# One step of a matmul order moved between two halves of a convolution, and an evacuation placed ahead of the last sine

## The chip, the cores and the metric

The kernel runs on one core of a Trainium2 chip. The metric is the device time of one execution in microseconds (us); the figure for the kernel before is the median of three runs. A separate, profiled execution gives the page and the trace that all readings come from.

## What is computed

The reference first runs a causal convolution along the sequence. Each of 8 heads has 7 taps, normalised by a softmax, and each head covers 24 of the 192 channels. Then comes a two-layer network with the activation h * cos(h):

```python
# x (8, 4096, 192), weight (8, 7); w = softmax(weight) along the taps
out = einsum('hk,bskhg->bshg', w, x_unf)     # x_unf: windows of 7 rows, zero-padded ahead
x = out.reshape(32768, 192)
h = x @ w_in                                  # 192 -> 2048, product 1
g = h * cos(h)
result = g @ w_out                            # 2048 -> 192, product 2
```

## The kernel before

The 32768 rows are worked in 64 tiles of 512 rows; two tiles make a unit of 1024 rows, for which rows are loaded and convolved together. All instructions are emitted in an order that is written out by hand, in strings of short tokens, one string per tile for TensorE (with what hangs on it) and one for ScalarE.

*Product 1.* `hJ` (J from 0 to 7) is `mm1`, line 405: six matmuls, 512 columns wide, that fill two banks of PSUM with a block `h`. TensorE's rows are split into two halves that work side by side, so matmuls come in pairs. The blocks come from a ring of three (`h_pool`), which the convolution shares.

*The activation.* `sJ` is `gcu`, lines 409 to 417: ScalarE writes the sine of h + pi/2 into `cs`, and VectorE multiplies it by `h` into `g`, which frees the block of the ring.

*Product 2.* `mN` emits N steps of `mm2_step`, line 452. A tile has 64 steps, of two matmuls each with 192 columns, one on each half of the rows. They run about one tile behind product 1. They add into two output banks, one for each pair of row blocks (`o_p` and `o_q`), and `q` and `p` mark the half and the end of a tile's 64 steps. At the half, the two row halves exchange banks.

*Evacuation.* `P` (ScalarE), and `Q` (VectorE) or `A` (ScalarE), copy the two output banks of the finished tile to `o_sb` (`evac`, line 470). `O` stores a tile whose two copies have been emitted (line 473), on SyncE's queue.

*The convolution.* In the steady order each tile convolves half of the heads of a unit ahead (`conv_part`, line 220; matmuls of line 196). `c1` emits four matmuls (two pairs), `c2` four more that add into the same two banks with the row halves exchanged. The second group must not start before the first has ended. This is done by a `Turn` (lines 163 to 174): an empty instruction on SyncE (seen in the profile as L168) waits for the first group, and the second group waits for it:

```python
            turn.mark(mm(1, 0), mm(3, 1))
            yield
            turn.wait(mm(2, 0), mm(0, 1))
```

`ec1` and `ec2` are ScalarE's copies of the two banks (line 211). `D` doubles the copied rows on GpSimd (line 264), `X` transposes them by DMA (line 275, SyncE's queue), `Y` mends the edges of the row blocks on GpSimd (lines 297 to 309), `K` casts loaded rows to bf16 on GpSimd (line 184), and `L` issues the loads of a unit (lines 75 and 69, SyncE's queue).

*Which tile uses which string.* Tiles 0 to 3 use `PE_FIRST` and `ACT_FIRST`, tiles 4 to 62 `PE_ORDER` and `ACT_ORDER`, and tile 63 `PE_LAST` and `ACT_LAST`. The convolution ends with tile 59; afterwards `c1` and `c2` emit nothing. A token of ScalarE's string is emitted as soon as it stands first and what it needs has been emitted on TensorE's side: `sJ` needs `hJ`, `P`, `Q` and `A` need `p`. In tile 63, product 2 of that tile itself starts with the `m7` after `h7`. Its 64 steps take row blocks in another order (`LAST_HALF`): 14 steps go to two blocks of the ring, 14 to the output banks `o_p` and `o_q`, then two and two for the last block of `g`, and then the second half.

Of the kernel before, what the change touches and what calls it, by code (L numbers as in the profile page):

```python
# [16 lines left out]
def kernel(  # L17
# [9 lines left out]
    B, S, D = x.shape  # L27
    H, K = weight.shape
# [191 lines left out]
    def conv_part(u, c, banks, whole=False):  # L220


        ps = banks()
        nb = UB + (u == 1)
        sides = [slice(0, 64), slice(64, 128)]

        def mm(i, rows, **flags):
            return conv_mm(u, c, ps, i, sides[rows], 0, nb, **{"start": False, "stop": False, **flags})

        if whole:  # L230
            for i in range(4):
                conv_mm(u, c, ps, i, slice(0, 128), 0, nb, start=i % 2 == 0, stop=i % 2 == 1)
            if u == 2 and c == 0:
                spread_taps(ps[1][:, UB * 2 * G : UB * 2 * G + K])
            yield
        else:
            mm(0, 0, start=True)
            mm(2, 1, start=True)
            turn = Turn()
# [3 lines that stand above are left out]
            mm(3, 0, stop=True)  # L243
            mm(1, 1, stop=True)
        yield
        if u not in ct_tiles:
            ct_tiles[u] = ct_pool.tile([128, UB + 1, NC, 2, 64], BF16, name="ct")
        for b in range(2):
            conv_out(u, c, ps, 0, 0, nb, nc.scalar.copy, banks=(b,))
            if b and u == 2 and c == 0:  # L250
                nc.scalar.copy(tap, ps[1][:, UB * 2 * G : UB * 2 * G + K])
            if b:
                have.add(("conv", u, c))
            yield
# [76 lines left out]
    for i, k in enumerate("DPDPDPDPDPDPDPAA"):  # L331
        q, rows = divmod(i, 4)
# [152 lines left out]

    PE_ORDER = "m11 h0 m4 h1 m6 h2 m7 q Y K h3 m7 h4 m7 c1 m3 c2 X L m6 h5 m9 p h6 D O h7 m4"
    ACT_ORDER = "s0 s1 s2 s3 s4 ec1 ec2 Q s5 P s6 s7"

    PE_FIRST = ["h0a L2 h0b h1 h2 h3 K1 W0 d11 d21 h4 h5 c11 W1 L3 c21 h6 h7 K2",
# [6 lines left out]
                "s0 s1 s2 s3 s4 Q s5 P s6 s7"]  # L498

    PE_LAST = "m10 h0 m3 h1 m13 h2 m2 q h3 m10 h4 m3 h5 m7 h6 m12 p h7 O m7"  # L500
    ACT_LAST = "s0 s1 s2 s3 s4 s5 s6 P s7 A"

    HALVES = {"": (0, NB), "a": (0, NB // 2), "b": (NB // 2, NB), "l": (0, NB // 2), "r": (NB // 2, NB)}
    conv = {}
# [4 lines left out]
    for t in range(NT + 1):  # L509
        u, second = divmod(t, TPU)  # L510
        cu = u + TPU
        if t >= 2 * TPU:
            conv["c"] = conv_part(cu, second, ring_banks) if cu < NU else iter(())
        pe = PE_LAST if t == NT - 1 else "m%d p" % (2 * STEPS * NT - step) if t == NT else PE_ORDER if t >= len(PE_FIRST) else PE_FIRST[t]
        act = ACT_LAST if t == NT - 1 else ACT_ORDER if t >= len(ACT_FIRST) else ACT_FIRST[t]
        act, h = act.split(), {}
# [95 lines left out]
```

## Time and profile before

| what | value |
|---|---|
| median of 3 runs | 714.65 us (714.59 to 715.40) |
| the profiled execution's own time | 715.43 us |
| its span on the core | 713.7 us |
| granted TensorE clock | 1.0 |
| TensorE matmuls, busy | 704.7 us (99%) |
| VectorE, busy | 638.4 us (89%) |
| ScalarE, busy | 599.3 us (84%) |
| GpSimd, busy | 303.4 us (43%) |
| matmuls of product 2 (L452), busy | 427.4 us, 8128 of 243 ns |
| matmuls of product 1 (L405), busy | 405.3 us, 3078 of 376 ns |
| matmuls of the convolution (L196), busy | 39.7 us, 472 of 245 ns |

The span runs from the first to the last instruction on the core; the execution's own time is longer by what lies around it. The durations of matmuls overlap each other, so the mean duration of one is several times its share of the time; the distance between the starts of two says what one costs. In the rows of a timeline stand the start and the length in us, the engine (PE is TensorE, PEld its weight loads, ACT ScalarE, DVE VectorE, POOL GpSimd, SP SyncE), the line of the kernel, the operation, what it writes and reads, and how many instructions the row merges; in square brackets stand idle time of the engine ahead of the row and who ended it.

### The profile page before, as it was taken

How to read it: one execution, taken by the hardware profiler on the slowest of the kernel's cores; microseconds unless marked ns; L12 is line 12 of the kernel's file. 1: busy time of each engine (PE TensorE's matmuls, PEld its weight loads, DVE VectorE, ACT ScalarE, POOL GpSimd, SP SyncE). 2: the span in 40 equal slices, each digit the busy share in tenths (PEclk: the TensorE clock that was granted, in tenths of full speed). 3: DMA queues.
4: the chain of work that ended last, by engine and by line, in shares of the span. 5: the costliest groups of instructions: out<-in, count | busy, mean ns of one | idle time of the engine just before them, and what ended most of it. 6: DMA issues, size and time to landing. Idle time of an engine off the chain costs nothing.

```text
span 713.7 us, 26519 instructions
## 1 busy us (share of the span) xinstructions
PE 704.7 (99%) x11826; PEld 512.3 (72%) x11826; DVE 638.4 (89%) x599; ACT 599.3 (84%) x717; POOL 303.4 (43%) x307
## 2 busy tenths in 40 slices
PE   8899999999999999999999999999999999999997
PEld 4677777777777777777777777777777777777776
DVE  6789998999899999989989989989998999999996
ACT  7788888888888888888888888888888888888875
POOL 6533554443553434544434544245544335532400
PEclk9999999999999999999999999999999999999999
DMA  9674445445356454355364465453453553643411
GB/s 234 165 197 71 125 120 146 97 123 138 94 134 145 79 141 119 101 145 127 93 146 89 130 146 106 113 138 101 127 145 84 136 111 114 141 95 76 96 46 46
DMA packets 183713, 85.25 MB, mean 119 GB/s; under 512 B 111664, under 2 KB 183216, under 8 KB 183600
## 3 DMA queue, kind: packets, MB, share of 16 engines
q1 hardware_dynamic: 182888, 82.59, 47.7%
q8 instruction: 92, 1.51, 0.9%
q0 software_dynamic: 416, 0.79, 0.6%
q10 hardware_dynamic: 296, 0.20, 0.1%
q14 instruction: 21, 0.17, 0.1%
HBM read 31.36 MB, written 25.17 MB: 79 GB/s over the span
## 4 chain that ended last, share of the span: by engine, by line
PE 96%; DVE 1%; ACT 1%; POOL 1%; issue 0%; POOLq 0%; DVEq 0%; SPq 0%
PE o_ps L452 47%; PE h L405 46%; PE h L196 3%; ACT cs L413 1%; DVE g L417 1%; POOL x_bf L184 0%; DVE band L333 0%; PE h L452 0%; PE h L363 0%; ACT ct L355 0%; ACT cT L366 0%; POOL w L85 0%; DVE diag L321 0%; ACT ct L211 0%; PE o_ps L349 0%
## 5 line engine op out<-in xcount | busy, mean ns | idle before, releaser
L417 DVE TENSOR_TENSOR g<-h,cs 128x1024 bf16<-128x1024 f32 (+1 forms) x513 | 599.8, 1216 | 18.5 <-ACT cs L413 16.6
L413 ACT ACTIVATE cs<-h 128x1024 bf16<-128x1024 f32 (+1 forms) x513 | 514.0, 1022 | 89.7 <-PE h L405 70.6
L452 PEld LDWEIGHTS <-g 64*128 64x128 bf16 x8192 | 353.3, 94 | 104.4 <-issue 0.6
L452 PE MATMUL o_ps<-wo,g 64*128 64x192 bf16 x8128 | 427.4, 243 | 0.2 <-ACT o_sb L470 0.2
L405 PE MATMUL h<-cT,w 64*128 64x512 bf16 (+1 forms) x3078 | 405.3, 376 | 1.4 <-DVE g L417 1.0
L405 PEld LDWEIGHTS <-w 64*128 64x128 bf16 x3078 | 144.2, 94 | 78.8 <-issue 3.1
L303 POOL TENSOR_TENSOR edge_prod<-cT,tap 128x1008 f32<-128x1008 bf16 x30 | 67.2, 2240 | 289.9 <-DMA cT<-ct 289.9
L184 POOL CAST x_bf<-x_f 128x1728 bf16<-128x1728 f32 (+2 forms) x33 | 80.8, 2448 | 59.6 <-DMA x_f<-in_x_dram 28.7
L470 DVE COPY o_sb<-o_ps 128x384 f32<-128x384 f32 x62 | 34.6, 558 | 45.2 <-PE o_ps L452 45.1
L211 ACT CAST ct<-h 128x384 bf16<-128x384 f32 x120 | 51.8, 482 | 11.9 <-PE h L196 11.8
L264 POOL COPY ct<-ct 128x1536 bf16<-128x1536 bf16 (+1 forms) x31 | 45.6, 1470 | 6.8 <-ACT ct L211 6.4
L196 PE MATMUL h<-x_bf,band 64*128 64x192 bf16 (+1 forms) x472 | 39.7, 245 | 1.6 <-POOL x_bf L184 1.4
L308 POOL TENSOR_TENSOR edge_prod<-edge_prod 128x144 f32<-128x144 f32 x60 | 33.3, 556 | 4.7
L306 POOL TENSOR_TENSOR edge_prod<-edge_prod 128x432 f32<-128x432 f32 x30 | 30.4, 1012 | 2.4
L470 ACT COPY o_sb<-o_ps 128x384 f32<-128x384 f32 x64 | 30.3, 473 | 0.5 <-PE o_ps L452 0.5
L196 PEld LDWEIGHTS <-band 64*128 64x128 bf16 (+1 forms) x480 | 18.5, 94 | 7.6 <-issue 2.6
L309 POOL TENSOR_TENSOR cT<-edge_prod 128x144 bf16<-128x144 f32 x30 | 18.3, 610 | 2.4
L266 POOL COPY ct<-x_bf 128x192 bf16<-128x192 bf16 x60 | 19.2, 350 | 0.0
L111 PE MATMUL o_ps<-zero 128*128 128x512 bf16 x12 | 5.5, 630 | 1.3 <-DVE zero L106 1.3
L95 POOL CAST wo<-wo_f 128x1536 bf16<-128x1536 f32 x2 | 2.9, 1470 | 2.6 <-DMA wo_f<-in_moe_w_out_dram 2.6
L111 PEld LDWEIGHTS <-zero 128*128 128x128 bf16 x12 | 1.5, 137 | 3.5 <-issue 2.2
L452 PE MATMUL h<-wo,g 64*128 64x192 bf16 x64 | 3.3, 243 | 0.0
(59 smaller groups left out, 40.5 us busy)
## 6 DMA issues: line engine op xcount, KB each, us to landing
out_dram<-o_sb SPq DMA_DIRECT2D x63, 384.0 KB
x_f<-in_x_dram SPq DMA_DIRECT2D x30, 768.0 KB
x_f<-in_x_dram SPq DMA_DIRECT2D x31, 96.0 KB
x_f<-in_x_dram SPq DMA_DIRECT2D x4, 384.0 KB
wo_f<-in_moe_w_out_dram SPq DMA_DIRECT2D x4, 384.0 KB
w<-in_moe_w_in_dram POOLq DMA_DIRECT2D x2, 384.0 KB, 6.3
cT<-ct SPq DMA_TRANSPOSE x32
out_dram<-o_sb ACTq DMA_DIRECT2D x2, 96.0 KB
```

The costliest lines, as they stand in the source:

```text
L184: copy(out=bf[u][:, n0 + o : n1 + o, :].rearrange("p n (h k r) -> p (n h) k r", k=NC, r=R), in_=x_tiles[u][:, n0:n1, :].rearrange("p n (h ...
L196: return nc.tensor.matmul(out=ps[i // 2][:, 0 : (n1 - n0) * 2 * G].rearrange("p (n k i r) -> p i n k r", n=n1 - n0, k=NC, i=2)[:, i % 2], ...
L211: copy(o[:, :, 0, :], i[:, :, 0, :])
L264: nc.gpsimd.tensor_copy(out=ct[:, 0:nb, :, 1, :], in_=ct[:, 0:nb, :, 0, :])
L303: nc.gpsimd.tensor_tensor(out=edge_prod, in0=window, in1=tap.rearrange("p (a b k) -> p a b k", a=1, b=1).to_broadcast([128, NC * UB, K - 1 ...
L306: nc.gpsimd.tensor_tensor(out=edge_prod[:, :, :, 0:3], in0=edge_prod[:, :, :, 0:3], in1=edge_prod[:, :, :, 3:6], op=ALU.add)
L308: nc.gpsimd.tensor_tensor(out=edge_prod[:, :, :, 0], in0=edge_prod[:, :, :, 0], in1=edge_prod[:, :, :, j], op=ALU.add)
L405: nc.tensor.matmul(out=h[:, i, n0 * 128 : n1 * 128], lhsT=w[rows, k, j, :], rhs=c[rows, m0 + n0 : m0 + n1, k, :], start=(k == 0), stop=(k ...
L413: nc.scalar.activation(out=cs[:, :, part], in_=h[:, :, part], func=AF.Sin, bias=math.pi / 2.0, scale=1.0)
L417: nc.vector.tensor_tensor(out=g_tiles[t][:, 2 * j : 2 * j + 2, part], in0=h[:, :, part], in1=cs[:, :, part], op=ALU.mult)
L452: ms.append(nc.tensor.matmul(out=o_ps[tt, b, si], lhsT=g_tiles[tt][rows, f, s * 128 : (s + 1) * 128], rhs=wo[rows, f // 2, f % 2, :], star ...
L470: (copy or copies[b])(o_sb[t][:, 2 * b : 2 * b + 2, :].rearrange("p s d -> p (s d)"), o_ps.pop((t, b)))
```

## The change

In TensorE's steady order, `c2` comes after four steps of product 2 instead of three, and five instead of six follow it ahead of `h5`. In ScalarE's order for the last tile, the evacuation `A` stands ahead of the sine `s7` instead of behind it, so that both evacuations are emitted at `p`, and `s7` after them at `h7`.

```diff
-    PE_ORDER = "m11 h0 m4 h1 m6 h2 m7 q Y K h3 m7 h4 m7 c1 m3 c2 X L m6 h5 m9 p h6 D O h7 m4"
+    PE_ORDER = "m11 h0 m4 h1 m6 h2 m7 q Y K h3 m7 h4 m7 c1 m4 c2 X L m5 h5 m9 p h6 D O h7 m4"
     ACT_ORDER = "s0 s1 s2 s3 s4 ec1 ec2 Q s5 P s6 s7"
...
     PE_LAST = "m10 h0 m3 h1 m13 h2 m2 q h3 m10 h4 m3 h5 m7 h6 m12 p h7 O m7"
-    ACT_LAST = "s0 s1 s2 s3 s4 s5 s6 P s7 A"
+    ACT_LAST = "s0 s1 s2 s3 s4 s5 s6 P A s7"
```

## The prediction

> **What bounds the kernel now.** The page comes first: the busy shares, the granted clock and the chain that ended last.
>
> ```profile
> PE 704.7 (99%) x11826; PEld 512.3 (72%) x11826; DVE 638.4 (89%) x599; ACT 599.3 (84%) x717; POOL 303.4 (43%) x307
> PEclk9999999999999999999999999999999999999999
> PE 96%; DVE 1%; ACT 1%; POOL 1%; issue 0%; POOLq 0%; DVEq 0%; SPq 0%
> ```
>
> TensorE carries 96% of the chain at full clock. Its busy share cannot show a stall, since matmuls overlap and their ends are modelled, so I went on to the spacing of matmul starts. In steady state a step of product 2 (one matmul on each half of the rows) follows the last after 82.5 ns: six steps of 0.66 us, less the 0.243 us that the last one takes, are five gaps of 0.083. I take 82.5 from the trace's nanosecond stamps. The timeline of one steady tile, TensorE's matmuls, its weight loads and ScalarE, around the conv's halves c1 (409.77) and c2 (410.20):
>
> ```profile
> 409.77 0.33 PE L196 MATMUL h<-x_bf,band 64*128 64x192 bf16 x4
> 409.94 0.41 PE L452 MATMUL o_ps<-wo,g 64*128 64x192 bf16 x6
> 410.20 0.34 PE L196 MATMUL h<-x_bf,band 64*128 64x192 bf16 x4
> 410.37 0.66 PE L452 MATMUL o_ps<-wo,g 64*128 64x192 bf16 x12
> 409.86 0.26 PEld L452 LDWEIGHTS <-g 64*128 64x128 bf16 x6
> 410.19 0.11 PEld L196 LDWEIGHTS <-band 64*128 64x128 bf16 x4
> 410.62 0.86 ACT L211 CAST ct<-h 128x384 bf16<-128x384 f32 x2 [0.20 <-PE h L196]
> 411.72 1.02 ACT L413 ACTIVATE cs<-h 128x1024 bf16<-128x1024 f32 x1 [0.24 <-PE h L405]
> ```
>
> c1 to the step after c2 is seven pairs, 7 x 82.5 = 0.578 us unhindered; the rows have 410.37 - 409.77 = 0.60. By the stamps c2's first pair is 15 ns late and its second comes after 93 ns in place of 82.5. The reason is in the weight loads: a load normally starts 81 ns ahead of its matmul, but c2's first starts at 410.195, 4 ns ahead. It waits for SyncE's answer to c1 (L168), which the list of waits does not charge to anybody because the engine looks busy. Summed over the 56 tiles that have this order and a conv (tiles 4 to 59), the first pairs lose 0.84 us and the second 0.59: 1.43 us. No other place in the steady order loses more than 1 ns at a time.
>
> How long the answer takes is seen where no step stands in between, in one of the opening tiles:
>
> ```profile
> 33.57 0.77 PE L196 MATMUL h<-x_bf,band 64*128 64x192 bf16 x8
> ```
>
> Eight matmuls, four pairs, should take 3 x 0.0825 + 0.243 = 0.49 us and take 0.77. From the last c1-type pair (33.655) to the first c2-type (33.997) are 0.342 us. The steady tile has the same: 409.854 to 410.199.
>
> The end of the kernel, in the timelines of ScalarE, TensorE and VectorE:
>
> ```profile
> 703.72 0.48 ACT L470 COPY o_sb<-o_ps 128x384 f32<-128x384 f32 x1
> 704.37 1.02 ACT L413 ACTIVATE cs<-h 128x1024 bf16<-128x1024 f32 x1 [0.17 <-PE h L405]
> 705.29 0.47 ACT L470 COPY o_sb<-o_ps 128x384 f32<-128x384 f32 x1
> 705.37 0.24 PE L452 MATMUL o_ps<-wo,g 64*128 64x192 bf16 x1
> 705.82 1.31 PE L452 MATMUL o_ps<-wo,g 64*128 64x192 bf16 x27 [0.20 <-ACT o_sb L470]
> 706.90 0.39 PE L452 MATMUL h<-wo,g 64*128 64x192 bf16 x4
> 707.39 0.34 PE L452 MATMUL h<-wo,g 64*128 64x192 bf16 x4
> 705.43 1.22 DVE L417 TENSOR_TENSOR g<-h,cs 128x1024 bf16<-128x1024 f32 x1 [0.29 <-ACT cs L413]
> ```
>
> P (703.72) empties one output bank, s7 (704.37) is the last sine, A (705.29) empties the other bank. TensorE needs that bank at 705.37 and stands until 705.82. At 706.90 it needs the product of s7 (VectorE, 705.43 to 706.65).
>
> **Part 1, the fourth step.** Nothing is added or removed; per tile one step (two matmuls) moves from behind c2 to ahead of it. With four steps c2's first pair is due 5 x 82.5 = 0.413 us after c1's last, and the answer allows 0.342: 70 ns to spare. Its load is due at 410.186 by the old tile's clock and the answer reaches it at 410.195, 9 ns late; a load 91 ns late cost 25 ns in all, so the first 66 ns of lateness are free. I take the whole loss as gone: -1.43 us. The other end, if lateness counted fully, is 9 ns x 56 = 0.50 us kept, so -0.93.
>
> The rule that speaks against this is in the Trainium skill, TensorE: Matmul & The Clock Gate, section LDWEIGHTS: a load takes its columns over 1.2 ns, 107 ns for 128. Were a matmul held until then, the load at 410.195 would put c2 at 410.302, 35 ns after its due 410.267, no better than the 25 ns lost today, and the sum would be part 2 alone. The row above has c2's matmul 4 ns after its load's start, so I do not follow it.
>
> What else moves: c2 ends 82.5 - 25.5 = 57 ns later against its surroundings and h5, five steps on, comes 25 ns earlier. ScalarE's two casts run from 410.68 to 411.54, the sine s5 is due at 411.70; today's 0.24 us of idle time there covers it and 0.16 stays. GpSimd's doubling of the conv's output starts 57 ns later, and its transposes leave only in the next tile, some 9 us on. The bank of c2's output is next taken by h7, at 412.91. The transposes X and loads L on SyncE's queue stand behind the answer to c1, whose time is unchanged. The moved step lies in the second half of a tile's product 2, for which all products g are long there. The tightest bank on the ring is h3's, free 0.21 us before TensorE takes it; its VectorE chain starts from h0, on the same side of c2, so the distance stays. Before tile 4 the two row halves run 20 ns apart, and c2's wait closes them to 3; without it they may stay apart, at no cost: h2 to h3 takes 1.22 us both at 59.99 (apart) and at 70.82 (closed).
>
> **Part 2, A ahead of s7.** P stays at 703.72. A can follow a copy after 0.376 us (the casts: 0.86 for two of 0.484), at 704.10; its bank is free by 704.58, far ahead of 705.37, so the stand until 705.82 goes. What is late next is s7. Start to start, a copy is followed by a sine after 0.359 us in the one place where nothing else holds it (33.55 to 33.91) and after 0.47 elsewhere, where the sine's matmul comes just then. So s7 starts at 704.46 to 704.57 in place of 704.37; I take 704.46, because the 0.47 rows are held by TensorE. Copies that don't overlap at all would make it 704.67. From there: 1.056 us to VectorE's start, 1.224 for its product, 0.057 to TensorE (as for the product before: end 705.142, matmul 705.199), so 706.80. TensorE alone would be there at 705.374 + 14 x 0.0825 = 706.53 and stands 0.27 us. Then four pairs, and the second half waits for SyncE's answer, 0.337 us after the later row half's second pair. Before, the halves ran 63 ns apart behind the stand, and that pair came at 707.050; now it comes at 706.80 + 0.083 + 0.003 = 706.89. The second half starts at 707.22 in place of 707.39: -0.17 us. With s7 at 704.67 it is 707.43, +0.04. The store behind A leaves SyncE 1.1 us earlier and frees that queue.
>
> The Trainium skill, ScalarE: Activation LUTs, section What ACT_TABLE_LOAD costs, lets instructions overlap by 93 ns: s7 would start at 704.49, part 2 give -0.14 and the sum be -1.57. The rows above overlap by 0.108 and 0.114, so I keep those.
>
> **Sum.** -1.43 - 0.17 = -1.60 us, all of it on TensorE's chain. The profiled execution took 715.43 (span 713.73, 1.70 around it), so it would take 713.83 with a span of 712.1. It stands 0.78 above the median of 714.65; the runs fall near 714.6 or near 715.4. Against the median: 713.05.
>
> **Rivals.**
> (1) The answer keeps part of its price: lateness of the weight load counts, 9 ns a tile by the stamps, up to the 25 ns of today. For it: no row shows a four-step distance. Against it: eight steps in an opening tile (37.5 to 38.26) leave c2 unhindered, and 66 ns of lateness are free today. -1.1 down to -0.2, so 713.55 to 714.5.
> (2) The order does not reach the timed runs: these spread over 0.8 us and a stall of 25 ns might be the recorder's. 714.5, by part 2 alone. Against it: 55 tiles in a row have 14.6 or 15.6 ns, and a stall of the same origin is 0.26 us where it is bare.
> (3) Slower: ScalarE becomes the chain. The casts behind c2 come 57 ns later, and s5, s6, s7 with them; if s5 had no room, each tile would grow by 57 ns rather than shrink, 56 x 0.057 = 3.2 us, 717.7. It decides where the idle time before s5 is under 0.08 us; the row has 0.24, and h0's bank, which waits for s5's product, is free 0.6 us early. So it is unlikely.
>
> **How the numbers follow.** A measurement of this kernel tells about 0.2% from no change, 1.43 us. The forecast has 0.82; its own spread (part 2 from -0.18 to +0.04, runs scattered as shown) leaves it beyond 1.43 us in three of four cases, 0.62, and within in 0.20. Rival 1 has 0.08 and rival 2 0.04, both within: 0.32 in all. Rival 3 has 0.06. The range goes from 712.6, the forecast with a median 0.4 low, to 714.1, which takes in part 2 as a loss, the upper group of runs and most of rival 1.
>
> **What would show it.** Right: from c1 to the first step after c2 (eight pairs) are 0.66 us, c2's weight loads start some 70 ns ahead of their matmuls, tile after tile in 10.79 us in place of 10.816; ScalarE idle before s5 is 0.16; at the end no stand at 705.4 less the shift, a shorter one ahead of the last product's steps. Wrong: c2 late by 10 ns or more in every tile; s5 released by ScalarE itself; s7 more than 0.3 us behind h7's end; or a new wait of TensorE on VectorE in the ring.

## The result, and the profile after

The changed kernel takes 713.40 us (median of 14 runs, 712.68 to 715.84) against 714.69 for the kernel before in the same session (14 runs). The ratio is 0.9982, with a 95% interval of 0.9973 to 0.9990: faster by 1.3 us, just inside the 0.2% that the prediction called the measurement's resolution. The prediction was 713.05, within 712.6 to 714.1. One run of 734.87 us (the evacuation alone, at a granted clock of 0.947) and one of 4218.91 us (the kernel before) stand apart from all others and are left out of the ratios.

The trace tells more than the timed runs, for the steady tiles repeat themselves closely: the five profiled executions with the changed steady order agree within 0.005 us over the whole stretch, and the two with the old one within 0.06. I cut each profiled execution at three matmuls: the first of c1 in tile 4, the first of h7 in tile 63, and the first of the last tile's second half of product 2.

| kernel (profiled execution) | opening | steady stretch | tail | rest | span | tile period |
|---|---|---|---|---|---|---|
| before | 63.66 | 639.85 | 3.88 | 6.34 | 713.73 | 10.816 |
| after | 62.81 | 638.41 | 3.76 | 6.29 | 711.26 | 10.790 |

The steady stretch loses 1.43 us and the tail 0.12. The other 0.9 us of the 2.46 between the two spans lie in the opening and the rest, where the change touches nothing: over all profiled executions of this case, the opening took between 62.7 and 63.7 us, whatever the kernel. The timed runs carry this scatter too.

The page of after has the same instructions and nearly the same chain:

```profile
PE 703.4 (99%) x11826; PEld 536.7 (75%) x11826; DVE 638.3 (90%) x599; ACT 599.2 (84%) x717; POOL 303.0 (43%) x307
PE 96%; DVE 2%; ACT 1%; POOL 1%; issue 0%; POOLq 0%; DVEq 0%; SPq 0%
```

The busy time of weight loads rose from 512 to 537 us with as many loads as before. The reader should not take that for work: the two row halves now run 18 to 20 ns apart in the whole steady stretch, where c2's wait used to close them to 3, so overlapping records cover more time.

A steady tile after, in the timelines of TensorE, its weight loads and ScalarE:

```profile
408.09 0.34 PE L196 MATMUL h<-x_bf,band 64*128 64x192 bf16 x4
408.25 0.51 PE L452 MATMUL o_ps<-wo,g 64*128 64x192 bf16 x8
408.58 0.34 PE L196 MATMUL h<-x_bf,band 64*128 64x192 bf16 x4
408.75 0.59 PE L452 MATMUL o_ps<-wo,g 64*128 64x192 bf16 x10
408.52 0.18 PEld L196 LDWEIGHTS <-band 64*128 64x128 bf16 x4
409.01 0.86 ACT L211 CAST ct<-h 128x384 bf16<-128x384 f32 x2 [0.26 <-PE h L196]
410.02 1.02 ACT L413 ACTIVATE cs<-h 128x1024 bf16<-128x1024 f32 x1 [0.15 <-PE h L405]
```

From c1 to the step behind c2 are 408.75 - 408.09 = 0.66 us for eight pairs: 82.5 ns each, no stall. c2's loads take 0.18 us from first to last in place of 0.11, the normal spacing. They start 62 ns ahead of their matmuls; before it was 4. ScalarE's idle time before s5 is 0.15.

The tail after, in the timelines of ScalarE, VectorE and TensorE:

```profile
701.44 0.86 ACT L470 COPY o_sb<-o_ps 128x384 f32<-128x384 f32 x2
702.18 1.04 ACT L413 ACTIVATE cs<-h 128x1024 bf16<-128x1024 f32 x1
703.26 1.23 DVE L417 TENSOR_TENSOR g<-h,cs 128x1024 bf16<-128x1024 f32 x1 [0.41 <-ACT cs L413]
703.08 1.32 PE L452 MATMUL o_ps<-wo,g 64*128 64x192 bf16 x28
704.54 0.34 PE L452 MATMUL h<-wo,g 64*128 64x192 bf16 x4
704.98 1.49 PE L452 MATMUL h<-wo,g 64*128 64x192 bf16 x32
```

P and A follow each other as one row, the output banks' 28 matmuls run through without a stand, and a shorter stand (0.30 us by the stamps) has appeared at 704.54, where TensorE waits for the product of s7.

### The profile page after: what moved, and what is told of

Same layout as the page of the kernel before. It is cut to its first block, busy times and chain, and to the rows that moved or that the text cites. A ratio compares the mean times of both kernels' runs of the same rounds, so it can differ in the third digit from the quotient of the medians.

```text
span 711.3 us, 26519 instructions
## 1 busy us (share of the span) xinstructions
PE 703.4 (99%) x11826; PEld 536.7 (75%) x11826; DVE 638.3 (90%) x599; ACT 599.2 (84%) x717; POOL 303.0 (43%) x307
## 4 chain that ended last, share of the span: by engine, by line
PE 96%; DVE 2%; ACT 1%; POOL 1%; issue 0%; POOLq 0%; DVEq 0%; SPq 0%
PE o_ps L452 46%; PE h L405 46%; PE h L196 3%; ACT cs L413 1%; DVE g L417 1%; POOL x_bf L184 0%; PE h L452 0%; DVE band L333 0%; PE h L363 0%; PE o_ps L375 0%; ACT ct L355 0%; POOL w L85 0%; DVE diag L321 0%; PE o_ps L349 0%; PE o_ps L125 0%
## 5 line engine op out<-in xcount | busy, mean ns | idle before, releaser
L452 PEld LDWEIGHTS <-g 64*128 64x128 bf16 x8192 | 367.3, 94 | 92.0 <-DVE g L417 0.6
L452 PE MATMUL o_ps<-wo,g 64*128 64x192 bf16 x8128 | 433.5, 243 | 0.0
L405 PE MATMUL h<-cT,w 64*128 64x512 bf16 (+1 forms) x3078 | 411.4, 376 | 1.5 <-DVE g L417 1.4
L405 PEld LDWEIGHTS <-w 64*128 64x128 bf16 x3078 | 159.2, 94 | 69.9 <-issue 3.0
L470 DVE COPY o_sb<-o_ps 128x384 f32<-128x384 f32 x62 | 34.6, 557 | 43.2 <-PE o_ps L452 43.0
L196 PE MATMUL h<-x_bf,band 64*128 64x192 bf16 (+1 forms) x472 | 40.8, 243 | 0.5 <-POOL x_bf L184 0.3
L470 ACT COPY o_sb<-o_ps 128x384 f32<-128x384 f32 x64 | 30.2, 473 | 0.5 <-PE o_ps L452 0.5
L196 PEld LDWEIGHTS <-band 64*128 64x128 bf16 (+1 forms) x480 | 22.8, 94 | 2.2 <-issue 1.4
```

The lines of the kernel that those rows point to most:

```text
L196: return nc.tensor.matmul(out=ps[i // 2][:, 0 : (n1 - n0) * 2 * G].rearrange("p (n k i r) -> p i n k r", n=n1 - n0, k=NC, i=2)[:, i % 2], ...
L405: nc.tensor.matmul(out=h[:, i, n0 * 128 : n1 * 128], lhsT=w[rows, k, j, :], rhs=c[rows, m0 + n0 : m0 + n1, k, :], start=(k == 0), stop=(k ...
L452: ms.append(nc.tensor.matmul(out=o_ps[tt, b, si], lhsT=g_tiles[tt][rows, f, s * 128 : (s + 1) * 128], rhs=wo[rows, f // 2, f % 2, :], star ...
L470: (copy or copies[b])(o_sb[t][:, 2 * b : 2 * b + 2, :].rearrange("p s d -> p (s d)"), o_ps.pop((t, b)))
```

## The experiments

**Each part alone.** The step alone:

```diff
-    ACT_LAST = "s0 s1 s2 s3 s4 s5 s6 P A s7"     # after
+    ACT_LAST = "s0 s1 s2 s3 s4 s5 s6 P s7 A"
```

> The fourth step alone; ScalarE's order of the last tile as before. My theory: the wait of c2 for SyncE's answer is the whole steady loss, so the steady stretch (start of the first conv half of tile 4 to start of h7 in tile 63; 639.85 us before, 638.41 after) is 638.41, and the tail (that h7 to the second half of the last tile's product 2; 3.88 before, 3.76 after) stays 3.88. Time against before: -1.43 us, ratio 0.998. Rival (the recorder's artefact): the stretch shortens in the trace, while the timed runs stand within 0.3 us of before.

Steady stretch 638.41 us, tail 3.88; timed 713.37 against 714.67, ratio 0.9979 (0.9970 to 0.9989). The timed runs show what the trace shows.

The evacuation alone:

```diff
-    PE_ORDER = "... c1 m4 c2 X L m5 h5 ..."      # after
+    PE_ORDER = "... c1 m3 c2 X L m6 h5 ..."
```

> The evacuation ahead of the last sine alone, three steps as before. My theory: steady stretch 639.85 us, tail 3.76 (-0.12), time against before -0.1, not to be told from no change by the timed runs. Rival (the gain of the tail is a by-product of the shorter tiles): tail 3.88.

Steady stretch 639.91, tail 3.76; timed 714.89 against 714.67, ratio 1.0001 (0.9992 to 1.0010). The steady stretch is 0.06 us longer than that of before in the same order, 1 ns a tile, which stays unexplained. Otherwise the two parts add up and don't touch each other. The tail's gain stands in the traces alone; the timed runs don't show it.

**How many steps the answer needs.** Fewer:

```diff
-    PE_ORDER = "... c1 m4 c2 X L m5 h5 ..."      # after
+    PE_ORDER = "... c1 m2 c2 X L m7 h5 ..."
```

> Two steps of product 2 between the halves in place of three or four, all else as after. My theory: the answer takes 0.342 us from c1's last pair, c2 is due 3 x 82.5 = 248 ns after it, so it comes 95 ns late, and its second pair 10 ns more; 0.105 x 56 = 5.9 us more than after, +4.3 us against before, and a tile period of 10.895 us. Rival (the artefact): no change of the timed runs.

Timed 719.34 against 714.67, ratio 1.0062 (1.0049 to 1.0076); period 10.899 us, steady stretch 644.51, 6.1 us more than after (5.9 expected). The timeline of its TensorE:

```profile
411.47 0.33 PE L196 MATMUL h<-x_bf,band 64*128 64x192 bf16 x4
411.64 0.33 PE L452 MATMUL o_ps<-wo,g 64*128 64x192 bf16 x4
411.90 0.34 PE L196 MATMUL h<-x_bf,band 64*128 64x192 bf16 x4
412.08 0.74 PE L452 MATMUL o_ps<-wo,g 64*128 64x192 bf16 x14
```

c1 to the step behind c2 takes 0.61 us for six pairs that need 0.495. The stall is real, and it grows with each step taken away as the answer's 0.342 us says.

More:

```diff
+    PE_ORDER = "... c1 m6 c2 X L m3 h5 ..."
```

> Six steps between the halves, all else as after. My theory: four steps already cover the answer with 70 ns to spare, so two more bring nothing: steady stretch 638.41 us, within 0.1 of after, -1.3 to -1.5 against before. Rival 1 of the prediction (a weight load that gets the answer 9 ns late still pays): 0.5 to 1.4 us shorter than after.

Steady stretch 638.413 us, to the nanosecond that of after; period 10.790; timed 713.16 against 714.67, ratio 0.9977 (0.9967 to 0.9988). Four steps had left nothing, though c2's loads come late with them and not with six. So rival 1 is out. One tile's c2 with six steps, in the timelines of TensorE's weight loads and TensorE:

```profile
409.16 0.20 PEld L196 LDWEIGHTS <-band 64*128 64x128 bf16 x4
409.24 0.34 PE L196 MATMUL h<-x_bf,band 64*128 64x192 bf16 x4
```

The loads start 81 ns ahead again.

**ScalarE as the chain.** All nine steps between the halves:

```diff
+    PE_ORDER = "... c1 m9 c2 X L h5 ..."
```

> All nine steps stand between the halves, so c2 comes directly ahead of h5, 0.41 us later than after the change. My theory: ScalarE's casts now end 0.25 us behind the time at which s5 is due, so s5 starts 0.25 us late and is released by ScalarE itself; behind it P frees the bank with some 0.14 us to spare and h0's block is free in time, so TensorE doesn't notice: steady stretch 638.41 us, as after. The slower rival of the prediction, in its plain form (any lateness of s5 lengthens the tile): 0.25 x 56 = 14 us more.

Steady stretch 638.48 us, period 10.791; timed 713.32 against 714.93, ratio 0.9977 (0.9968 to 0.9987). Its ScalarE:

```profile
410.11 0.86 ACT L211 CAST ct<-h 128x384 bf16<-128x384 f32 x2 [0.67 <-PE h L196]
410.85 1.04 ACT L413 ACTIVATE cs<-h 128x1024 bf16<-128x1024 f32 x1
411.76 0.50 ACT L470 COPY o_sb<-o_ps 128x384 f32<-128x384 f32 x1
```

The sine s5 has no bracket any more: ScalarE's own casts release it. h5 has ended its matmuls by then and s5 is late, and TensorE still loses nothing in nearly every tile: the distances from one c1 to the next are 10.789 to 10.791 us but for the last one, 10.853. There (tile 58) ScalarE's casts start 0.28 us later than two tiles earlier, P moves with them, and TensorE starts the next tile's product 2, which waits for P, 0.065 us late. That one wait is the whole difference of 0.06 us to after.

c2 behind h5 and five more steps:

```diff
+    PE_ORDER = "... c1 m9 h5 m5 c2 X L m4 p h6 ..."
```

> The conv's second half is put behind h5 and five further steps, so c2 comes about 1.5 us later than after the change and ScalarE's casts hold s5 back by about 1.25 us. My theory: this is the point from which the slower rival decides; P, behind s5 on ScalarE, frees the bank about 0.85 us after TensorE wants it, and the tile grows by 0.8 to 0.9 us, 45 to 50 us in all; TensorE's wait is for ScalarE's P. Rival (ScalarE has room for this too): 638.4 us in the steady stretch.

Steady stretch 684.40 us, 46.0 more; period 11.612, 0.82 more; one timed run, 759.91. In its timelines:

```profile
414.45 0.86 ACT L211 CAST ct<-h 128x384 bf16<-128x384 f32 x2 [1.73 <-PE h L196]
416.12 0.50 ACT L470 COPY o_sb<-o_ps 128x384 f32<-128x384 f32 x1
416.67 1.41 PE L452 MATMUL o_ps<-wo,g 64*128 64x192 bf16 x30 [0.48 <-ACT o_sb L470]
```

The slower rival exists, at its expected price, and the wait ends with P (L470): it decides where P frees the bank late, not where s5 loses its idle time.

**What is late next in the tail.** The last sine and its product in halves of the columns:

```diff
-    ACT_LAST = "s0 s1 s2 s3 s4 s5 s6 P A s7"     # after
+    ACT_LAST = "s0 s1 s2 s3 s4 s5 s6 P A s7l s7r"
```

> The last sine and its product in two halves of the columns, all else as after. My theory: what is late next in the tail is s7 and its product (TensorE stands 0.30 us for it at the last block's steps); in halves VectorE starts 0.4 us earlier and ends about when TensorE comes: tail 3.46 to 3.50 us in place of 3.76; steady stretch 638.41; timed runs 0.3 us shorter than after, less than they can tell. Rival (the stand is not the product's but the exchange of banks): tail 3.76.

Tail 4.15 us, longer by 0.39; neither theory had that. Timed 713.98 against 714.93, ratio 0.9985 (0.9976 to 0.9993). ScalarE's timeline:

```profile
702.91 0.62 ACT L413 ACTIVATE cs<-h 128x512 bf16<-128x512 f32 x1
704.28 0.60 ACT L413 ACTIVATE cs<-h 128x512 bf16<-128x512 f32 x1 [0.76 <-DVE g L417]
```

The second half sine waits for the first half product. So both half sines went first:

```diff
...
+        for part, cs in halves:
+            nc.scalar.activation(out=cs[:, :, part], in_=h[:, :, part], func=AF.Sin, bias=math.pi / 2.0, scale=1.0)
+        for part, cs in halves:
+            nc.vector.tensor_tensor(out=g_tiles[t][:, 2 * j : 2 * j + 2, part], in0=h[:, :, part], in1=cs[:, :, part], op=ALU.mult)
```

> The split of the last sine once more, with both half sines ahead of both half products, since in the last attempt the second half sine waited for the first half product. My theory: half sines at 0 and 0.6 us, VectorE starts 0.4 us earlier and its second half ends as TensorE comes: tail 3.46 to 3.50 us, in place of 3.76 after the change; steady stretch 638.41. Rival (the first half product now waits for the second half sine): tail about 3.9.

Tail 3.88; timed 713.42 against 714.89, ratio 0.9988 (0.9978 to 0.9998); it is nearer to 1 than the two medians because three of the twelve runs took 715.4 to 716.2. In its timelines of ScalarE and VectorE:

```profile
702.26 1.10 ACT L426 ACTIVATE cs<-h 128x512 bf16<-128x512 f32 x2
703.40 1.29 DVE L428 TENSOR_TENSOR g<-h,cs 128x512 bf16<-128x512 f32 x2 [0.47 <-ACT cs L426]
```

VectorE starts when both half sines have ended (703.36): the rival. In both orders whichever engine comes second on the block `h` of PSUM waits for the one before it, halves or not. I take it that the two reads of one block are ordered as whole blocks, but no run separates this from an order that comes by the `cs` buffers. In both, TensorE's stand follows the time of the last product, so the exchange of banks is not what holds it there.

**The same wait where something else stands behind it.** In an opening tile, whose bare wait of 0.26 us gave the prediction its 0.342:

```diff
-                "... h5 m6 p d22 h6 d13 d23 m8 h7 m13",     # after
+                "... h5 m6 p d22 h6 d13 m4 d23 m4 h7 m13",
```

> In the opening tile in which two halves of a conv follow each other with no step between (TensorE stands 0.263 us), four steps are put between them and four behind, in place of eight behind; all else as after. My theory: this wait goes too, but TensorE waits for VectorE at h7 right behind it (0.13 us) and again at 49.9 us (0.25 us), so the time comes back there: from the first of these halves to the first conv half of tile 4 it is 30.10 us before and after the change, and I expect 30.0 to 30.1. Rival (every wait taken from TensorE is gained, as in the steady tiles): 29.83.

From the first of these halves to c1 of tile 4: 30.096 us, as after. Its TensorE:

```profile
32.90 0.33 PE L196 MATMUL h<-x_bf,band 64*128 64x192 bf16 x4
33.41 0.51 PE L452 MATMUL o_ps<-wo,g 64*128 64x192 bf16 x8 [0.18 <-ACT o_sb L470]
33.73 0.34 PE L196 MATMUL h<-x_bf,band 64*128 64x192 bf16 x4
```

The time did come back, but sooner than I said: the four steps themselves wait for P's copy (by the stamps 0.34 us late at 33.41), and h7 still waits for VectorE behind that. By h7 this tile and that of after are level: 1.397 us from the first half in both. Same edit, same cover, no gain.

**No answer at all.** The steady conv on all 128 rows:

```diff
-            conv["c"] = conv_part(cu, second, ring_banks) if cu < NU else iter(())
+            conv["c"] = conv_part(cu, second, ring_banks, True) if cu < NU else iter(())
```

> In the steady tiles the conv uses all 128 rows in four matmuls instead of two groups of four half-row matmuls, so that there is no answer to wait for; c1 emits all and c2 nothing; all else as after. The columns are the same, 4 x 82.5 ns. My theory: what the steps between the halves hide is the answer alone, so without one the tile is as long as with four steps, 10.790 us, unless loading weights for all rows has to wait for the matmuls ahead: then up to 0.1 us a tile more, 5 us. Rival (there is more to gain than the change got): under 10.78 us a tile.

Timed 725.82 against 714.93, ratio 1.0152 (1.0138 to 1.0166); period 11.003 us, 0.213 more a tile, twice the bound that I had set. So both theories missed. Its matmuls and weight loads:

```profile
415.36 0.50 PE L196 MATMUL h<-x_bf,band 128*128 128x192 bf16 x4
415.80 0.92 PE L452 MATMUL o_ps<-wo,g 64*128 64x192 bf16 x18
415.36 0.28 PEld L196 LDWEIGHTS <-band 128*128 128x128 bf16 x4 [0.16 <-issue]
415.80 0.28 PEld L452 LDWEIGHTS <-g 64*128 64x128 bf16 x8 [0.16 <-issue]
```

The loads stand idle 0.16 us at each change between half rows and all rows, and by the stamps TensorE starts 0.095 us late at the first and 0.097 at the second; the matmul behind each comes 10 ns late besides. In half rows with four steps the conv costs its columns and nothing else.

## Why the prediction was right, point by point

- *The loss of 1.43 us, and that the fourth step takes all of it.* Measured 1.43 in the steady stretch, by both the change and the step alone. The busy share (99% before and after) and the list of waits would have shown neither the loss nor the gain; the distance of starts did.
- *The answer's 0.342 us.* With two steps c2's loads start 0.338 us and its matmuls 0.342 after c1's last pair; four steps cover that, three don't, and six bring no more.
- *9 ns of lateness are free.* They were, and more: the loads were late by up to 20 ns, since the row halves stayed apart, and the stretch was the same as with six steps. The prediction's 66 free ns were reckoned too low. Where c2 waits for the answer (before, and with two steps), its matmuls start 4 ns after their loads instead of 81, so 77 ns can go before the first pair is late; the 10 ns of the second pair come on top (25 in all before). The prediction weighed a rule against its row: the Trainium skill (TensorE: Matmul & The Clock Gate, section LDWEIGHTS) gives a load of 128 columns 107 ns. The loads of L196 are recorded here with 92 to 99 ns, and c2 started 62 ns after its load's start, so no matmul was held until its load had ended. The page gives the length of a load alone; that a matmul must wait for its end was the prediction's reading. The row was the right side to take.
- *The row halves stay apart at no cost.* They did, 18 to 20 ns from tile 4 on, with the period at 10.790.
- *The cover behind c2.* ScalarE's idle time before s5 was forecast at 0.16 and is 0.15.
- *The tail.* Forecast -0.17, measured -0.12. s7 started 0.747 us after P (0.74 forecast), with 0.37 us from copy to sine for 0.36. The 0.05 lie mostly in two terms that were a little short. From s7's start to VectorE's are 1.074 us, not 1.056, since a sine right behind a copy takes 1.04 rather than 1.02. From the product's first step to the second half are 0.438, not 0.423: the halves ran 3 ns apart as forecast, but the second pair behind the stand came after 93 ns rather than 83, as c2's second pair did before, and the answer took 0.342 us rather than 0.337. The new stand of 0.30 us (0.27 forecast) is the product's.
- *The sum.* -1.60 was forecast, the two stretches give -1.55, the medians -1.3, for the step alone as for the whole change. The last difference isn't settled by a mechanism; it is within the scatter of the opening. The chance of 0.62 for more than 0.2% was too high for a sum that stood only 0.17 us beyond that mark.
- *The rivals.* Rival 1 fell with six steps, rival 2 with the timed runs of the single step and of two steps. Rival 3 was rightly held unlikely, but its point was misplaced: the prediction let it decide when the idle time before s5 is gone, and with nine steps it is gone and all tiles but one keep their length. ScalarE has further room behind s5, and the point is where P frees its bank too late.
- *The range.* Its width came from the scatter of the runs and the end of part 2. The median lies 0.35 above the forecast; 0.05 of that is part 2, so what was needed was room for the scatter. That the median fell inside was the width's doing, not the sum's precision.

## What to carry to other kernels

When an engine is 99% busy, compare the starts of its instructions with their steady spacing; a stall of 25 ns that repeats in every tile is invisible in busy shares and waits, but can be counted to the nanosecond. Find the same wait somewhere without cover to learn its full length, then put just enough work between question and answer. Before counting the gain, look for the next wait behind it: here the same edit gained 1.43 us in the steady tiles and nothing in an opening tile.

## What the runs showed of the hardware

- A matmul can start 4 ns after its weight load has started (81 ns in the steady order); the next pair then comes after 93 ns in place of 82.5. Loads that started 62 ns ahead cost nothing.
- A change of the array from half rows to all rows and back cost 0.21 us for the two ways, with the loads idle 0.16 us at each.
- A sine directly behind a copy on ScalarE started 0.36 to 0.38 us after the copy's start, though the copy's record has 0.47 to 0.50.
